# Hash attention and token mixing on one core: block sums moved ahead of the weight conversion, first loads moved behind the first hash bits, a square moved to a later step

## The chip, the core and the metric
The kernel runs on one core of one Trainium2 chip. The metric is the time of one execution on the device in microseconds (us), as a median over runs. A core has TensorE (PE: matrix products, with PEld for its weight loads), VectorE (DVE), ScalarE (ACT), GpSimd (POOL) and SyncE (SP), which here only issues DMA transfers. Each works through its own queue in order; they meet through semaphores.

## The reference, cut to what matters
Attention in which a query sees only keys of the same hash bucket, and behind it a mixer over tokens and channels:

```python
q_bits = (q @ proj > 0); k_bits = (k @ proj > 0)        # 6 bits each
mask = bucket(q_bits)[:, :, :, None] == bucket(k_bits)[:, :, None, :]
scores = where(mask, q @ k.T / sqrt(64), -1e9)
x = softmax(scores) @ v                                  # (4, 768, 8 heads * 64)
h = relu(x.T @ w_tok1) @ w_tok2                          # mixing over tokens
u = x + h.T
out = u + relu(u @ w_ch1) @ w_ch2                        # mixing over channels
```

Batch 4, 8 heads, 768 tokens, head dimension 64. The weights come as 64-bit numbers; the kernel turns their words into float32 itself.

## The kernel before
Two heads of one batch make a *pair*; there are 16 pairs, and a pair is done in two *halves* of 384 queries (`Half`). One (pair, half) is a *block* here. Keys come in six chunks of 128. Scores stand with the keys in the partitions, so that the sum over keys is a product with a matrix of ones.

A block on TensorE: `scores(0)` gives chunks 0 to 2 (`sc`, a product of q and k, and on top of it one of the hash bits, which makes the scores of other buckets hugely negative), `weigh(1)` is the older block's last three products with v (`acc`), `scores(1)` gives chunks 3 to 5, `weigh(0)` the first three products with v, and then the older block's `divide` makes its sums over keys (`sums`). ScalarE turns each chunk into `e` (exponential), sums up v for a small correction (`add_values`, tiles `vt`, `vsum`) and copies `acc` to `num`. The six `e` of a block are added before `sums`: GpSimd makes `esa` (e0 + e1); VectorE makes `esd` from e3, e4, e5 (`add(0)`) and then adds e2 and `esa` (`add(1)`). VectorE then takes the reciprocal `den` of `sums`, and GpSimd multiplies it with `num` into `XT`.

Once per pair, in its first half, `hashes(n + 1)` makes the next pair's bits: four products of q and k with `projblk` (`hp`), a comparison and a scaling on VectorE (`g`), and eight small DMAs that put the bits where the scores read them (`bits`). `hp` and `sums` share one PSUM buffer (tag `sm`, `bufs=1`), so the one product waits until VectorE has read the other.

From pair 1 on, each block also does one third of the conversion of a weight tile (`weights.some`): *begin* (ScalarE converts the low words, VectorE puts together `big` from the high words, two operations), *join* (one VectorE operation, ScalarE's square of the high words, two GpSimd products) and *end* (one VectorE operation, which writes the weight). Eight tiles are done in the attention, in blocks 2 to 25; with the thirds and halves the same step comes back after six blocks. The rest is converted in the mixer, where `weights.one` does all three steps in one call, the end being that of the tile before.

The order of each engine's work is the order of the code (`manual_schedule`). The loop that sets it is short:

```python
now.scores(0)
if before: before.weigh(1)
if half == 0: load(n + 2); hashes(n + 1)
if before: before.add(0)
now.scores(1)
if half == 0: add_values(n + 1)
if n: weights.some(third)
now.weigh(0)
if before: before.add(1); before.divide()
```

After the attention, `mix1(b)` turns x of batch b with transposes on TensorE (`trp`, two PSUM buffers) and copies on ScalarE (`turn`), and multiplies with `w_tok1` (`t`); `mix2(b)` multiplies with `w_tok2`, and VectorE adds into `XT`. From about 500 us on there is only the channel mixing.

Of the kernel before, what the change touches and what calls it, by code (L numbers as in the profile page):

```python
# [32 lines left out]
F32 = mybir.dt.float32  # L33
# [4 lines left out]
ALU = mybir.AluOpType  # L38
ACT = mybir.ActivationFunctionType
# [5 lines left out]
def kernel(  # L45
# [12 lines left out]
    nc = tc.nc  # L58
    P = 128
    B, NP, _, _, S = qk.shape  # L60
    D = 64
    NB = proj.shape[1]
# [7 lines left out]
    HALF = S // 2  # L70
# [6 lines left out]
    BIG = 2.0**20  # L77
# [10 lines left out]
    ones = const.tile([P, D], F32, name="ones")  # L88
    nc.vector.memset(ones, 1.0)

    projblk = const.tile([P, 32], F32, name="projblk")
    nc.vector.memset(projblk, 0.0)
    for i in range(2):
        nc.sync.dma_start(out=projblk[D * i : D * i + D, 16 * i : 16 * i + NB], in_=proj)


    bitscale = const.tile([P, 1], F32, name="bitscale")
    nc.gpsimd.memset(bitscale, BIG)
    nc.gpsimd.memset(bitscale[:64], 1.0)
    for j in range(2, 4):  # L100
        for i in range(2):
            nc.gpsimd.affine_select(
                out=bitscale, in_=bitscale, compare_op=ALU.not_equal, fill=-NB * BIG,
                base=-(32 * j + 16 * i + NB), pattern=[[0, 1]], channel_multiplier=1,
            )
    largest = const.tile([P, B * NP], F32, name="largest")
    unsafe = const.tile([1, 1], I32, name="unsafe")

# [14 lines left out]
    class Conversion:  # L123
# [48 lines left out]
        def join(self):  # L172
            if not self.begun:
                return
            raw, tmp, to, rows = self.begun
            self.begun = None
            lo, hi = raw[:, :, 0].bitcast(F32), raw[:, :, 1].bitcast(F32)
            big, unit = tmp[:, 0], tmp[:, 1]
            nc.vector.tensor_scalar(
                unit.bitcast(U32), big.bitcast(U32), 0xFF800000, None, op0=ALU.bitwise_and,  # L180
            )
            nc.scalar.activation(hi, hi, ACT.Square)
            nc.gpsimd.tensor_tensor(unit, unit, lo, op=ALU.mult)  # L183
            nc.gpsimd.tensor_tensor(big, big, unit, op=ALU.add)  # L184
            self.ready = hi, big, to, rows

        def end(self):

            if not self.ready:
                return  # L190
            size, big, to, rows = self.ready
            self.ready = None
            nc.vector.scalar_tensor_tensor(
                to, size.rearrange("p (t n) -> p t n", t=rows), LEAST * LEAST,
                big.rearrange("p (t n) -> p t n", t=rows), op0=ALU.is_ge, op1=ALU.mult,
            )
# [17 lines left out]
    pairs = [(b, hp) for b in range(B) for hp in range(NP)]  # L214

    def turn(b, x, bank):

        for r in range(0, NR, 2):
            ps = bank()
            for k in range(2):  # L220
                at = S * b + P * (r + k)
                for cb in range(NCB):
                    nc.tensor.transpose(ps[:, k, P * cb : P * cb + P], XT[:, cb, at : at + P], ident)
            nc.scalar.copy(x[:, r : r + 2], ps)


    def attention(pool, psum):
        zeroed = [pool.tile([P, 2, S], BF16, name=f"bits{n}", tag=f"bits{n}", bufs=1) for n in range(3)]
        loaded = {}

        def load(n):
            if n >= len(pairs):
                return
            b, hp = pairs[n]
            t = pool.tile([P, 2, S], F32, name="qk", tag="qk", bufs=3)
            if n:
                nc.sync.dma_start(out=t, in_=qk[b, hp])
            else:
                for half in range(2):
                    sl = slice(HALF * half, HALF * half + HALF)  # L240
                    nc.sync.dma_start(out=t[:, :, sl], in_=qk[b, hp, :, :, sl])
            vn = pool.tile([P, 2, NR, D], F32, name="vn", tag="vn", bufs=3)
            nc.sync.dma_start(out=vn, in_=v[b, hp])
            vt = pool.tile([P, S], F32, name="vt", tag="vt", bufs=2)
            nc.sync.dma_start(out=vt, in_=vT[b, hp])
            loaded[n] = [t, vn, vt, None]

        def add_values(n):

            vt = loaded[n][2]  # L250
            vsum = pool.tile([P, 1], F32, name="vsum", tag="vsum", bufs=4)
            nc.scalar.activation(vt, vt, ACT.Copy, scale=EPS, accum_out=vsum)
            loaded[n][3] = vsum

        def hashes(n):

            g = pool.tile([P, HALF], BF16, name="g", tag="g", bufs=2)
            ps = psum.tile([P, 512], F32, name="hp", tag="sm", bufs=1)
            for j in (0, 2, 1, 3):
                sl = slice(HALF * (j % 2), HALF * (j % 2) + HALF)  # L260
                nc.tensor.matmul(  # L261
                    ps[32 * j : 32 * j + 32, :HALF], projblk, loaded[n][0][:, j // 2, sl],
                    start=True, stop=True,
                )
            nc.vector.tensor_scalar(g, ps[:, :HALF], 0.0, 0.5, op0=ALU.is_gt, op1=ALU.subtract)
            nc.vector.tensor_scalar(g, g, bitscale, None, op0=ALU.mult)
            for j in (0, 2, 1, 3):
                sl = slice(HALF * (j % 2), HALF * (j % 2) + HALF)
                for i in range(2):
                    at = 32 * j + 16 * i  # L270
                    issuer = nc.scalar if n == 0 and j >= 2 else nc.sync
                    issuer.dma_start(
                        out=zeroed[n % 3][D * i : D * i + NB + 1, j // 2, sl], in_=g[at : at + NB + 1],
                    )

        def scores(n, half, chunks):
# [46 lines left out]
            at = S * b + HALF * half  # L323
            nc.gpsimd.tensor_tensor(XT[:, hp, at : at + HALF], num, den, op=ALU.mult)  # L324

        for n in range(2):
            load(n)
        for t in zeroed:
            nc.gpsimd.memset(t, 0.0)
        weights = Conversion(  # L330
            pool,
            [(w_tok1, W1, 3, (0, NR)), (w_tok2, W2, 1, (0, NJ)), (w_ch1, WC1, 1, (0, NCB // 2))],
            bufs=1,
        )
        hashes(0)
        add_values(0)
        half = None

        class Half:

# [7 lines left out]
            def weigh(self, g):  # L348
                if g == 0:
                    self.acc = psum.tile([P, 512], F32, name="acc", tag="acc", bufs=1)  # L350
                chunks = range(GR * g, GR * g + GR)
                weigh(self.n, self.acc, self.es[GR * g :], chunks)
                if g == 0:
                    self.a = pool.tile([P, 2, HALF], F32, name="esa", tag="esa", bufs=2)
                    nc.gpsimd.tensor_tensor(self.a, self.es[0], self.es[1], op=ALU.add)  # L355
                else:
                    self.num = pool.tile([P, HALF], F32, name="num", tag="num", bufs=3)
                    nc.scalar.activation(
                        self.num, self.acc[:, :HALF], ACT.Identity, bias=loaded[self.n][3],
                    )  # L360

            def add(self, k):

                es = self.es
                if k == 0:
                    self.d = pool.tile([P, 2, HALF], F32, name="esd", tag="esd", bufs=2)
                    nc.vector.tensor_tensor(self.d, es[3], es[4], op=ALU.add)  # L367
                    nc.vector.tensor_tensor(self.d, self.d, es[5], op=ALU.add)  # L368
                else:
                    nc.vector.tensor_tensor(self.d, self.d, es[2], op=ALU.add)  # L370
                    nc.vector.scalar_tensor_tensor(  # L371
                        self.d, self.d, NR * EPS, self.a, op0=ALU.add, op1=ALU.add,
                    )
# [6 lines left out]
        for n in range(len(pairs)):  # L380
            for half in range(2):
                now = Half(n, half)

                now.scores(0)
                if before:
                    before.weigh(1)
                if half == 0:
                    load(n + 2)
                    if n + 1 < len(pairs):
                        hashes(n + 1)  # L390
                if before:
                    before.add(0)

                now.scores(1)
                if half == 0 and n + 1 < len(pairs):
                    add_values(n + 1)
                if n:
                    weights.some(third)
                    third = (third + 1) % 3
                now.weigh(0)  # L400
                if before:
                    before.add(1)
                    before.divide()
                before = now
        while third or weights.fetched:
            weights.some(third)
            third = (third + 1) % 3
        before.weigh(1)
        before.add(0)
        before.add(1)  # L410
        turn(0, x0, lambda: psum.tile([P, 2, 512], F32, name="trp", tag="sc", bufs=3))
        before.divide()

# [231 lines left out]
```

## Time and profile before

| | us |
|---|---|
| median of three runs (lowest, highest) | 999.64 (999.03, 1001.22) |
| the profiled execution, its own time | 1003.09 |
| its span from first to last instruction | 1001.3 |
| TensorE busy | 946.6 (95%) |
| VectorE busy | 386.1 |
| ScalarE busy | 278.2 |
| GpSimd busy | 197.4 |
| mean granted clock of TensorE | 0.981 of full |

The span is that of one profiled execution, whose own time includes what lies around it. The profile names instructions by the line of the kernel (L285), the engine and the tiles. A wait is put down to the instruction that released it. A granted clock of 1.00 is 2.4 GHz and 0.50 is 1.2 GHz; a number between them is a mean over a stretch that had both.

### The profile page before, as it was taken

The page shows a single profiled execution, that of the slowest core. Times are in us where ns is not written, and L with a number is a line of the kernel's source. Part 1 is how long each engine was busy: PE and PEld are TensorE (multiplying, and loading weights), DVE is VectorE, ACT ScalarE, POOL GpSimd, SP SyncE. Part 2 cuts the span into 40 slices and gives each one's busy share as a digit, 9 for nine tenths or more (in the row PEclk, how much of TensorE's full clock was granted, in tenths as well). Part 3 has the DMA queues.
Part 4 walks back from the last instruction along what each step waited for, and adds up shares of the span by engine and source line. Part 5 has one row for each costly group of instructions (what it writes and reads, how often), then busy time and mean ns, then how long its engine had stood idle before and what let it go on. Part 6 is the DMA issues. An engine that isn't in the chain of part 4 may idle for free.

```text
span 1001.3 us, 9101 instructions
## 1 busy us (share of the span) xinstructions
PE 946.6 (95%) x3649; PEld 423.4 (42%) x3649; DVE 386.1 (39%) x349; ACT 278.2 (28%) x389; POOL 197.4 (20%) x119
## 2 busy tenths in 40 slices
PE   6998998999999997988999999999999999999997
PEld 2443343333333443445544444444444444444443
DVE  1577777777777787477400030020002003000000
ACT  3555554545554552433111011001001001100100
POOL 2144254334525232554200000000000000000000
PEclk8999999999999998998999999999999999999999
DMA  6121222232231011232000030030012003000000
GB/s 223 67 93 69 97 97 68 103 120 91 71 100 65 31 34 63 85 104 95 1 0 1 31 136 1 21 142 6 11 46 112 10 22 136 0 22 21 1 11 34
DMA packets 20513, 61.12 MB, mean 61 GB/s; under 512 B 2800, under 2 KB 4208, under 8 KB 20464
## 3 DMA queue, kind: packets, MB, share of 16 engines
q1 hardware_dynamic: 20408, 60.45, 17.3%
q8 instruction: 30, 0.49, 0.2%
q14 instruction: 19, 0.16, 0.1%
q10 hardware_dynamic: 56, 0.02, 0.0%
HBM read 53.48 MB, written 6.29 MB: 60 GB/s over the span
## 4 chain that ended last, share of the span: by engine, by line
PE 83%; DVE 12%; ACT 1%; issue 1%; DMA 1%; SPq 0%; DVEq 0%; ACTq 0%
PE c L552 25%; PE c L542 25%; PE sc L285 12%; PE acc L310 8%; PE t L513 5%; PE t L526 4%; PE sums L320 3%; DVE esd L371 3%; DVE den L322 2%; DVE esd L370 2%; DVE esd L368 2%; DVE tmp L164 1%; PE hp L261 1%; DVE tmp L167 1%; DVE esd L367 1%
## 5 line engine op out<-in xcount | busy, mean ns | idle before, releaser
L552 PE MATMUL c<-r,WC 128*128 128x512 f32 x576 | 248.2, 592 | 0.0
L542 PE MATMUL c<-XT,WC 128*128 128x512 f32 x576 | 248.2, 592 | 0.0
L302 ACT ACTIVATE e<-sc 128x768 f32<-128x768 f32 x192 | 153.1, 811 | 130.1 <-PE sc L285 128.1
L556 DVE TENSOR_TENSOR o<-c,XT 128x512 f32<-128x512 f32 x24 | 16.6, 692 | 425.4 <-PE c L552 425.4
L285 PE MATMUL sc<-qk 64*128 64x384 f32 x768 | 168.6, 519 | 0.0
L552 PEld LDWEIGHTS c<-r,WC 128*128 128x128 f32 x576 | 109.4, 190 | 137.8 <-issue 137.8
L542 PEld LDWEIGHTS c<-XT,WC 128*128 128x128 f32 x576 | 109.4, 190 | 137.1 <-issue 136.6
L547 ACT ACTIVATE r<-c 128x512 f32<-128x512 f32 x72 | 43.0, 598 | 430.4 <-PE c L542 430.4
L310 PE MATMUL acc<-e,vn 128*64 128x384 f32 x768 | 137.9, 494 | 0.0
L322 DVE RECIPROCAL den<-sums 128x384 f32<-128x384 f32 x32 | 81.9, 2558 | 47.8 <-PE sums L320 47.8
L285 PEld LDWEIGHTS sc<-qk 64*128 64x128 f32 x768 | 68.0, 194 | 71.2 <-issue 55.1
L310 PEld LDWEIGHTS acc<-e,vn 128*64 128x64 f32 x768 | 49.5, 136 | 76.4 <-issue 76.4
L324 POOL TENSOR_TENSOR XT<-num,den 128x384 f32<-128x384 f32 x32 | 40.7, 1272 | 197.0 <-ACT e L302 166.9
L355 POOL TENSOR_TENSOR esa<-e 128x768 f32<-128x768 f32 x32 | 66.4, 2076 | 19.3 <-ACT e L302 19.2
L285 PE MATMUL sc<-bits 64*128 64x384 bf16 x384 | 65.1, 332 | 4.7 <-DMA bits<-g 4.6
L183 POOL TENSOR_TENSOR tmp<-tmp,raw 128x768 f32<-128x768 f32 x20 | 44.0, 2202 | 68.7 <-ACT raw L162 32.4
L320 PE MATMUL sums<-esd,ones 128*64 128x384 f32 x128 | 27.5, 505 | 26.8 <-DVE esd L371 26.7
L513 PE MATMUL t<-x,W 128*128 128x512 f32 x96 | 47.3, 654 | 2.7 <-DVE den L322 2.7
L371 DVE SCALAR_TENSOR_TENSOR esd<-esd,esa 128x768 f32<-128x768 f32 x32 | 42.3, 1322 | 3.3
L184 POOL TENSOR_TENSOR tmp<-tmp 128x768 f32<-128x768 f32 x20 | 42.0, 2099 | 1.6
L368 DVE TENSOR_TENSOR esd<-esd,e 128x768 f32<-128x768 f32 x32 | 41.0, 1280 | 3.3
L526 PE MATMUL t<-W,r 128*128 128x384 f32 x128 | 41.8, 486 | 0.0
(44 smaller groups left out, 425.2 us busy)
## 6 DMA issues: line engine op xcount, KB each, us to landing
raw<-in_moe_w_ch SPq DMA_DIRECT2D x16, 768.0 KB
seen<-in_qk SPq DMA_DIRECT2D x16, 768.0 KB
qk<-in_qk SPq DMA_DIRECT2D x15, 768.0 KB
vn<-in_v SPq DMA_DIRECT2D x16, 384.0 KB
vt<-in_vT SPq DMA_DIRECT2D x16, 384.0 KB
out<-o SPq DMA_DIRECT2D x24, 256.0 KB
raw<-in_moe_w_tok SPq DMA_DIRECT2D x4, 768.0 KB
bits<-g SPq DMA_DIRECT2D x124, 5.2 KB
```

Of the source, the lines that this page charges most:

```text
L285: nc.tensor.matmul(sc[c][:, i, :HALF], t[rows, 1, P * c : P * c + P], t[rows, 0, qs], start=first, stop=not first,)
L302: nc.scalar.activation(e, sc[c][:, :, :HALF], ACT.Exp, scale=SCALE)
L310: nc.tensor.matmul(acc[D * i : D * i + D, :HALF], vn[:, i, c], e[:, i], start=(c == 0), stop=(c == NR - 1),)
L320: nc.tensor.matmul(ps[D * i : D * i + D, :HALF], ones, total[:, i], start=True, stop=True)
L322: nc.vector.reciprocal(den, ps[:, :HALF])
L355: nc.gpsimd.tensor_tensor(self.a, self.es[0], self.es[1], op=ALU.add)
L368: nc.vector.tensor_tensor(self.d, self.d, es[5], op=ALU.add)
L371: nc.vector.scalar_tensor_tensor(self.d, self.d, NR * EPS, self.a, op0=ALU.add, op1=ALU.add,)
L513: nc.tensor.matmul(ps, W1[:, r, P * j : P * j + P], x[:, r], start=(r == 0), stop=(r == NR - 1),)
L526: nc.tensor.matmul(ps[:, :HALF], r1[:, j, P * cb : P * cb + P], W2[:, j, HALF * half : HALF * half + HALF], start=(j == 0), stop=(j == NJ ...
L542: nc.tensor.matmul(ps, WC1[:, cb, P * t : P * t + P], XT[:, cb, sl], start=(cb == 0), stop=(cb == NCB - 1),)
L552: nc.tensor.matmul(ps, WC2[:, t, P * cb : P * cb + P], r2[t], start=(t == 0), stop=(t == NHT - 1),)
```

## The change
Four things move; no arithmetic changes.

- In a block, the four adds of the older block's `esd` come ahead of the weight step: the two of `add(1)` (formerly `add(0)`) behind `weigh(1)`, the two of `add(2)` behind `scores(1)`. GpSimd's `esa`, now `add(0)`, is issued behind `scores(1)` too, ahead of GpSimd's part of the weight step.
- `hashes(n + 1)` comes behind the weight step instead of behind `weigh(1)`.
- At the start, `projblk` is issued by ScalarE behind a first small exponential (`warm`), the loads of v for pair 0 and all loads for pair 1 come behind pair 0's hash bits, and pair 0's bits are made and issued in two parts, first those of the first half of the tokens.
- ScalarE's square of the high words moves from *join* to *end*.

```diff
-        nc.sync.dma_start(out=projblk[D * i : D * i + D, 16 * i : 16 * i + NB], in_=proj)
+        nc.scalar.dma_start(out=projblk[D * i : D * i + D, 16 * i : 16 * i + NB], in_=proj)
...
         # Conversion.join
-            nc.scalar.activation(hi, hi, ACT.Square)
             nc.gpsimd.tensor_tensor(unit, unit, lo, op=ALU.mult)
             nc.gpsimd.tensor_tensor(big, big, unit, op=ALU.add)
...
         # Conversion.end
             self.ready = None
+            nc.scalar.activation(size, size, ACT.Square)
             nc.vector.scalar_tensor_tensor(
...
         # hashes
-            for j in (0, 2, 1, 3):
-                sl = slice(HALF * (j % 2), HALF * (j % 2) + HALF)
+            for j in range(4):
+                sl = slice(HALF * (j // 2), HALF * (j // 2) + HALF)
...
-            nc.vector.tensor_scalar(g, ps[:, :HALF], 0.0, 0.5, op0=ALU.is_gt, op1=ALU.subtract)
-            nc.vector.tensor_scalar(g, g, bitscale, None, op0=ALU.mult)
+            for rows in [slice(0, 64), slice(64, P)] if n == 0 else [slice(0, P)]:
+                nc.vector.tensor_scalar(
+                    g[rows], ps[rows, :HALF], 0.0, 0.5, op0=ALU.is_gt, op1=ALU.subtract,
+                )
+                nc.vector.tensor_scalar(g[rows], g[rows], bitscale[rows], None, op0=ALU.mult)
...
-                    issuer = nc.scalar if n == 0 and j >= 2 else nc.sync
+                    issuer = nc.scalar if n == 0 and i else nc.sync
...
-        for n in range(2):
-            load(n)
+        warm = pool.tile([P, 1], F32, name="warm", tag="warm", bufs=1)
+        nc.scalar.activation(warm, ones[:, :1], ACT.Exp)
+        load_qk(0)
         for t in zeroed:
             nc.gpsimd.memset(t, 0.0)
+        hashes(0)
+        load_v(0)
+        load_qk(1)
+        load_v(1)
+        add_values(0)
...
-        hashes(0)
-        add_values(0)
...
                 now.scores(0)
                 if before:
                     before.weigh(1)
+                    before.add(1)
                 if half == 0:
-                    load(n + 2)
-                    if n + 1 < len(pairs):
-                        hashes(n + 1)
-                if before:
-                    before.add(0)
+                    load_qk(n + 2)
+                    load_v(n + 2)
                 now.scores(1)
+                if before:
+                    before.add(2)
+                now.add(0)
                 if half == 0 and n + 1 < len(pairs):
                     add_values(n + 1)
                 if n:
                     weights.some(third)
                     third = (third + 1) % 3
+                if half == 0 and n + 1 < len(pairs):
+                    hashes(n + 1)
                 now.weigh(0)
                 if before:
-                    before.add(1)
                     before.divide()
```

VectorE in a first half with an *end* step, before and then after the change (`esd` are the adds, `W_86` and `W_87` the weight that the step writes, `g` the hash bits):

```order
L322 RECIPROCAL den<-sums 128x384
L265 TENSOR_SCALAR g<-hp 128x384
L266 TENSOR_SCALAR g<-g,bitscale 128x384
L367 TENSOR_TENSOR esd<-e 128x768
L368 TENSOR_TENSOR esd<-esd,e 128x768
L193 SCALAR_TENSOR_TENSOR W_86<-raw,tmp 128x768
L370 TENSOR_TENSOR esd<-esd,e 128x768
L371 SCALAR_TENSOR_TENSOR esd<-esd,esa 128x768
```

```order
L329 RECIPROCAL den<-sums 128x384
L378 TENSOR_TENSOR esd<-e 128x768
L379 TENSOR_TENSOR esd<-esd,e 128x768
L381 TENSOR_TENSOR esd<-esd,e 128x768
L382 SCALAR_TENSOR_TENSOR esd<-esd,esa 128x768
L195 SCALAR_TENSOR_TENSOR W_87<-raw,tmp 128x768
L270 TENSOR_SCALAR g<-hp 128x384
L273 TENSOR_SCALAR g<-g,bitscale 128x384
```

The hash bits went from the front of the block to its end, and the weight step from between the adds to behind them.

ScalarE in the mixer, from the second call of `one` in `mix2(0)` to the copies of x for batch 2, before and then after (`raw` are the words of a tile; L162 and L164 convert the low ones, L182 and L194 square the high ones):

```order
L162 ACTIVATE raw_2954<-raw_2954 128x768
L182 ACTIVATE raw_2954<-raw_2954 128x768
L162 ACTIVATE raw_2973<-raw_2973 128x768
L182 ACTIVATE raw_2973<-raw_2973 128x768
L224 COPY x0_89<-trp_3029 128x1024
```

```order
L164 ACTIVATE raw_2958<-raw_2958 128x768
L194 ACTIVATE raw_2908<-raw_2908 128x768
L164 ACTIVATE raw_2977<-raw_2977 128x768
L194 ACTIVATE raw_2958<-raw_2958 128x768
L226 COPY x0_90<-trp_3033 128x1024
```

The last square ahead of the copies was that of the tile just begun, and is now that of the tile before it.

SyncE's transfers at the start, before and then after:

```order
L241 DMA qk<-in_qk 128x2x384
L94 DMA projblk<-in_proj 64x6 x2
L241 DMA qk<-in_qk 128x2x384
L243 DMA vn<-in_v 128x768
L245 DMA vt<-in_vT 128x768
L237 DMA qk<-in_qk 128x1536
L243 DMA vn<-in_v 128x768
L245 DMA vt<-in_vT 128x768
L151 DMA raw<-in_moe_w_tok 128x3x512
L272 DMA bits_99<-g 7x384 x4
```

```order
L239 DMA qk<-in_qk 128x2x384 x2
L279 DMA bits_100<-g 7x384 x4
L247 DMA vn<-in_v 128x768
L249 DMA vt<-in_vT 128x768
L239 DMA qk<-in_qk 128x1536
L247 DMA vn<-in_v 128x768
L249 DMA vt<-in_vT 128x768
L153 DMA raw<-in_moe_w_tok 128x3x512
```

The four bits that SyncE issues for pair 0 stood behind six further loads and a weight, and now stand in front of them; `projblk` is gone from this queue.

## Rows read from the trace of the kernel before
**Rows 1.** Waits of TensorE: for whom, us in total, times, longest.
```profile
PE sums L320 <- DVE esd L371: 26.7, 19, 2.6
```
**Rows 2.** Busy time of each engine in stretches (start:end, length), granted clock, DMA.
```profile
34.37:382.16 347.79, 323.54 (x2032) 137.71 (x2034) 260.70 (x210) 185.71 (x254) 138.44 (x76) 0.98 0.23 78
...
362.14:372.20 10.06, 10.06 (x67) 4.46 (x65) 8.34 (x5) 5.40 (x7) 4.00 (x2) 1.00 0.00 0
166.43:178.19 11.76, 11.76 (x67) 5.18 (x65) 9.25 (x6) 5.45 (x7) 6.50 (x4) 0.85 0.26 83
```
**Rows 3.** The chain that ended last, 36 to 42 us: start, us, what.
```profile
39.08 0.78 PE hp L261 x8
```
**Rows 4.** VectorE in order of time, of three blocks: start, us, instruction, idle before.
```profile
39.93 0.56 DVE L265 TENSOR_SCALAR g<-hp 128x384 bf16<-128x384 f32 x1 [2.95 <-PE hp L261]
...
42.69 0.56 DVE L164 TENSOR_SCALAR tmp<-raw 128x768 uint32<-128x768 uint32 x1
43.28 0.96 DVE L167 SCALAR_TENSOR_TENSOR tmp<-raw,tmp 128x768 uint32<-128x768 uint32 x1
...
138.34 0.95 DVE L193 SCALAR_TENSOR_TENSOR W<-raw,tmp 128x768 f32<-128x768 f32 x1
...
379.96 0.96 DVE L371 SCALAR_TENSOR_TENSOR esd<-esd,esa 128x768 f32<-128x768 f32 x1
```
**Rows 5.** TensorE in order of time, end of pair 15's first half.
```profile
371.45 0.81 PE L320 MATMUL sums<-esd,ones 128*64 128x384 f32 x4
```
**Rows 6.** GpSimd in order of time, a block with a join.
```profile
125.64 2.44 POOL L183 TENSOR_TENSOR tmp<-tmp,raw 128x768 f32<-128x768 f32 x1 [1.42 <-ACT num L358]
```
**Rows 7.** ScalarE in order of time, in pair 1's first half and in the mixing.
```profile
43.29 0.83 ACT L252 ACTIVATE vt<-vt 128x768 f32<-128x768 f32 x1
...
434.97 0.92 ACT L182 ACTIVATE raw<-raw 128x768 f32<-128x768 f32 x1 [4.72 <-DVE tmp L167]
```
**Rows 8.** TensorE in order of time, in the token mixing.
```profile
409.85 1.09 PE L223 MATMUL trp<-ident,XT 128*128 128x128 f32 x8 [1.44 <-ACT x L224]
410.78 10.46 PE L513 MATMUL t<-x,W 128*128 128x512 f32 x24
...
436.82 1.97 PE L223 MATMUL trp<-ident,XT 128*128 128x128 f32 x8 [3.51 <-ACT x L224]
438.59 11.18 PE L513 MATMUL t<-x,W 128*128 128x512 f32 x24
...
467.12 12.26 PE L513 MATMUL t<-x,W 128*128 128x512 f32 x24
```
**Rows 9.** TensorE in order of time, at the start.
```profile
5.16 3.10 PE L261 MATMUL hp<-qk,projblk 128*32 128x384 f32 x8 [5.16 <-DMA projblk<-in_proj]
...
18.93 1.52 PE L285 MATMUL sc<-qk 64*128 64x384 f32 x4
```
**Rows 10.** SyncE's queue in order of time, at the start.
```profile
1.53 1.22 SPq L94 DMA_DIRECT2D projblk<-in_proj  x2
2.79 0.60 SPq L241 DMA_DIRECT2D qk<-in_qk  x1
...
20.54 5.90 SPq L272 DMA_DIRECT2D bits<-g  x8
```
**Rows 11.** ScalarE in order of time, at the start.
```profile
12.99 1.28 ACT L252 ACT_TABLE_LOAD   x1 [12.99 <-DMA bits<-g]
14.29 0.84 ACT L252 ACTIVATE vt<-vt 128x768 f32<-128x768 f32 x1
...
16.95 2.21 ACT L302 ACTIVATE e<-sc 128x768 f32<-128x768 f32 x3 [1.73 <-PE sc L285]
```
**Rows 12.** TensorE's weight loads in order of time, at the start.
```profile
6.77 0.19 PEld L261 LDWEIGHTS hp<-qk,projblk 128*32 128x32 f32 x4 [1.43 <-DMA qk<-in_qk]
```
**Rows 13.** Busy time of each engine from 10 to 14 us; last, DMA share and GB/s.
```profile
10.00:14.00 4.00, 1.25 (x8) 0.38 (x4) 0.00 (x0) 1.01 (x1) 0.00 (x0) 0.92 1.02 401
```
**Rows 14.** The chain that ended last, 4 to 17 us.
```profile
12.67 3.73 DMA bits<-g
```

More of the change, by code (lines that the diff above doesn't have):

```diff
@@ L93 @@
     for i in range(2):
-        nc.sync.dma_start(out=projblk[D * i : D * i + D, 16 * i : 16 * i + NB], in_=proj)
+        nc.scalar.dma_start(out=projblk[D * i : D * i + D, 16 * i : 16 * i + NB], in_=proj)
     bitscale = const.tile([P, 1], F32, name="bitscale")
     nc.gpsimd.memset(bitscale, BIG)
[L99 to L105, printed above, removed]
+    for j in range(4):
+        if j % 2 == 0:
+            nc.gpsimd.memset(bitscale[32 * j : 32 * j + 32], 1.0)
+        else:
+            for i in range(2):
+                nc.gpsimd.affine_select(
+                    out=bitscale, in_=bitscale, compare_op=ALU.not_equal, fill=-NB * BIG,
+                    base=-(32 * j + 16 * i + NB), pattern=[[0, 1]], channel_multiplier=1,
+                )
     largest = const.tile([P, B * NP], F32, name="largest")
@@ L229, in attention, with load_qk @@
         loaded = {}
-        def load(n):
+        def load_qk(n):
             if n >= len(pairs):
@@ L235, in load, with load_v @@
             t = pool.tile([P, 2, S], F32, name="qk", tag="qk", bufs=3)
[L236 to L241, printed above, removed]
+            for sl in [slice(0, HALF), slice(HALF, S)] if n == 0 else [slice(0, S)]:
+                nc.sync.dma_start(out=t[:, :, sl], in_=qk[b, hp, :, :, sl])
+            loaded[n] = [t, None, None, None]
+        def load_v(n):
+            if n >= len(pairs):
+                return
+            b, hp = pairs[n]
             vn = pool.tile([P, 2, NR, D], F32, name="vn", tag="vn", bufs=3)
@@ L258, in hashes @@
             ps = psum.tile([P, 512], F32, name="hp", tag="sm", bufs=1)
-            for j in (0, 2, 1, 3):
-                sl = slice(HALF * (j % 2), HALF * (j % 2) + HALF)
+            for j in range(4):
+                sl = slice(HALF * (j // 2), HALF * (j // 2) + HALF)
                 nc.tensor.matmul(
-                    ps[32 * j : 32 * j + 32, :HALF], projblk, loaded[n][0][:, j // 2, sl],
+                    ps[32 * j : 32 * j + 32, :HALF], projblk, loaded[n][0][:, j % 2, sl],
                     start=True, stop=True,
                 )
-            nc.vector.tensor_scalar(g, ps[:, :HALF], 0.0, 0.5, op0=ALU.is_gt, op1=ALU.subtract)
-            nc.vector.tensor_scalar(g, g, bitscale, None, op0=ALU.mult)
-            for j in (0, 2, 1, 3):
-                sl = slice(HALF * (j % 2), HALF * (j % 2) + HALF)
+            for rows in [slice(0, 64), slice(64, P)] if n == 0 else [slice(0, P)]:
+                nc.vector.tensor_scalar(
+                    g[rows], ps[rows, :HALF], 0.0, 0.5, op0=ALU.is_gt, op1=ALU.subtract,
+                )
+                nc.vector.tensor_scalar(g[rows], g[rows], bitscale[rows], None, op0=ALU.mult)
+            for j in range(4):
+                sl = slice(HALF * (j // 2), HALF * (j // 2) + HALF)
                 for i in range(2):
                     at = 32 * j + 16 * i
-                    issuer = nc.scalar if n == 0 and j >= 2 else nc.sync
+                    issuer = nc.scalar if n == 0 and i else nc.sync
                     issuer.dma_start(
-                        out=zeroed[n % 3][D * i : D * i + NB + 1, j // 2, sl], in_=g[at : at + NB + 1],
+                        out=zeroed[n % 3][D * i : D * i + NB + 1, j % 2, sl], in_=g[at : at + NB + 1],
                     )
@@ L334, in attention @@
         )
-        hashes(0)
-        add_values(0)
-        half = None
         class Half:
@@ L352, in weigh @@
                 weigh(self.n, self.acc, self.es[GR * g :], chunks)
[L353 to L356, printed above, removed]
+                if g == 1:
                     self.num = pool.tile([P, HALF], F32, name="num", tag="num", bufs=3)
@@ L365, in add @@
                 if k == 0:
+                    self.a = pool.tile([P, 2, HALF], F32, name="esa", tag="esa", bufs=2)
+                    nc.gpsimd.tensor_tensor(self.a, es[0], es[1], op=ALU.add)
+                elif k == 1:
                     self.d = pool.tile([P, 2, HALF], F32, name="esd", tag="esd", bufs=2)
@@ L386, in attention @@
                     before.weigh(1)
+                    before.add(1)
                 if half == 0:
-                    load(n + 2)
-                    if n + 1 < len(pairs):
-                        hashes(n + 1)
+                    load_qk(n + 2)
+                    load_v(n + 2)
+                now.scores(1)
                 if before:
-                    before.add(0)
-                now.scores(1)
+                    before.add(2)
+                now.add(0)
                 if half == 0 and n + 1 < len(pairs):
@@ L408, in attention @@
         before.weigh(1)
-        before.add(0)
         before.add(1)
+        before.add(2)
         turn(0, x0, lambda: psum.tile([P, 2, 512], F32, name="trp", tag="sc", bufs=3))
```

2 lines of the change are left out of this document (1 added, 1 removed).

## The prediction
> **What bounds the kernel now.** I read in this order: the waits of TensorE, the stretches between block starts, VectorE's, GpSimd's and ScalarE's rows inside a block, the token mixing, and the start. TensorE is the engine of the chain nearly everywhere; from 500 us on it hardly pauses, so only its idle time before that can be won. Its longest sum of waits is 26.7 us, in 19 waits of the `sums` products for VectorE's last add [rows 1].
>
> A *block* is one (pair, half). An undisturbed one lasts 10.06 us [rows 2]; with the hash products of the next pair, 0.78 [rows 3], it is 10.84. From pair 1 to the last products of pair 15, 34.37 to 382.16, are 347.8 us [rows 2]. Undisturbed they would be 14 halves with hashes at 10.84 and 16 without at 10.06, 312.7 in all. So 35.1 us are waits and what follows them: after some waits TensorE is granted 0.85 of its clock over a block, which then lasts 11.76, 1.7 more [rows 2]; a part of it runs at 1.2 GHz.
>
> **Why the sum is late.** In a first half VectorE sits idle 2.95 us for the hash products although the older block's exponentials lie ready; then come hash bits, two adds, a weight operation, two adds [rows 4]. All four adds must end before `sums`.
>
> **The new order in a block, pairs 1 to 12.** I count from the start of a block's scores. VectorE does the reciprocal, then all four adds at once. What that costs with GpSimd's work in between can be read: in the last pair no weight is converted and no hash waits, so its second half already runs reciprocal and four adds in this order, collisions with GpSimd included. There the last add ends at 379.96 + 0.96 = 380.92, in a block begun at 372.20: 8.7 us in [rows 2, 4]. `sums` begins at 371.45, 0.75 before the next block [rows 5, 2], so it is due at 9.3 in a second half and 10.1 in a first. The adds end in time, and what may now hold `sums` is the comparison of the hash products (L270): both use one PSUM buffer, and the comparison stands behind the weight operation. By thirds:
> - First half, *begin*: two word operations, 1.55 [rows 4], to 10.2; the comparison 0.56 [rows 4], to 10.75. `sums` waits 0.65.
> - First half, *join*: one short operation; the comparison ends before 10.1. No wait. But GpSimd now starts two products, the first 2.44 [rows 6]; the scaling of the bits waits for it, so the next reciprocal starts 0.7 late, and the following second half runs some 0.2 over.
> - First half, *end*: L195 now needs ScalarE's square from the same block. ScalarE does three exponentials, then `vt`, which starts at 43.29, 8.9 in; 0.78 of this was for hash products that now come later [rows 7, 3], so 8.1, to 9.0. The square takes 0.92 [rows 7], to 10.0; L195 0.95, to 11.0; the comparison to 11.6 [rows 4]. `sums` waits 1.55.
> - Second halves: 8.7 against 9.3, no wait but the 0.2 above. Their weight operation falls into VectorE's idle time before the next reciprocal.
>
> Six blocks hold each third once in a first and once in a second half: 0.65 + 1.55 + 0.2 = 2.4. Four such rounds are 9.6. In pairs 13 to 15, 8.7 plus 0.56 is before 10.1: no wait. So 347.8 becomes 312.7 + 9.6 = 322.3, **25.5 less.** Bounds: 35 if none of the new waits shows; 10 if the eight waits of the first halves are twice as long (8.8) and four of them cost the slower clock (6.8). I take the middle, since it is made of rows that already hold the new order.
>
> **Squares in the mixing.** Now ScalarE's square of a word waits 4.7 us for VectorE's L167, which reads the same words [rows 7]; the copies of the transposed `x` queue behind it, and TensorE's third bank of transposes waits 3.5 for them [rows 8]. This happens twice alike, for x of batches 2 and 3. After the change the square is that of the call before, whose words L167 has read long since, and the copies start as soon as the first bank is full: 2 x 3.5, less 0.2. The eight transposes behind the wait take 1.97 where they took 1.09, and 24 products 11.18 and 12.26 for 10.46 [rows 8]: 2 x 0.88 + 0.72 + 1.80 = 4.3 more. Batch 1's wait of 1.44 [rows 8] stays, for a square is still queued at that place. **11.1 less.** What grows: the last word operation waits for the square, and the first adds of `mix2` stand behind it, some 2 us later than now; four PSUM banks cover that. If they don't, it costs 1 to 3. Bounds 7 to 11; nothing at all is a rival below.
>
> **The start.** `projblk` now comes from ScalarE behind a table load and an activation. It was used at 5.16 [rows 9], 2.4 after its last issue's end (1.53 + 1.22) [rows 10]. An estimate: ScalarE's load from 0.75, 1.28 long [rows 11], an activation of 0.2, two issues of some 0.75, so 3.7, and 2.4 more: 6.1. The hash products take 3.1 [rows 9]; their first half's bits can be issued from 8.7 on, the last ones until 11.6, and no longer queue behind loads. But `vn` and `vt` of pair 0 are issued behind them, and ScalarE's first exponential stands behind `vt`'s sum. A load of 384 KB took 4.0 from issue (2.79) to use (6.77) [rows 10, 12]; one more of that size takes 1.0 at 401 GB/s [rows 13]. Issued from 11.65, `vt` is there at 16.7, its sum (0.84) ends at 17.6, and the exponentials start at 17.75 where they started at 16.95 [rows 11]. TensorE goes on at 18.55, 0.4 before the 18.93 of now [rows 9], with 2.6 of scores and then 0.8 of hash products, which now precede those scores. It will have stood idle some 5 us, as now, and then its clock was half. Between 0.2 gained (full clock) and 2.2 lost (half clock throughout) I take **1.5 lost**, because the idle stretch is as long as that of now.
> The Trainium skill ("ScalarE: Activation LUTs", *What ACT_TABLE_LOAD costs*) puts a drain of about 1.38 us behind a load of 1.28. By it the start would lose 2.9 and the kernel take 1.4 more. The trace shows the 1.28, but the next activation at 14.29, 0.02 after the load's end, so no drain there [rows 11].
>
> **Sum.** 25.5 + 11.1 - 1.5 = 35.1. The profiled execution took 1003.1, 3.5 above the median of three runs, 999.6; no stage here explains this difference, so I take the 35.1 from both: 968.0 for a profile, **964.5 as a median.** About 0.2% (2 us) can be told from no change.
>
> **Rivals.**
> - *The waits come back in another place* (15%): the new waits of 1.55 drop the clock each time, or VectorE and GpSimd collide otherwise than in pair 15. For it: the slow block of [rows 2] stood behind a wait. Against it: the adds, which caused the waits, have 0.6 to 1.4 us in hand. Price 6.8 for the clock alone, 15.6 with the waits doubled: 971 to 980, say 974.
> - *The mixing gains nothing* (10%): the word operation behind the square holds the adds, and so PSUM, as long as the copies waited before. 975.6.
> - *The table load holds ScalarE longer* (5%): by one more stretch of 1.28, which delays `projblk` and all behind it. 965.8.
> - *The hash bits come too late* (4%), the way to a slower kernel. They are now issued at the end of a first half, not in its middle. After a *join* their scaling ends 11.65 in; the last of eight issues (5.9 in all) starts 5.2 later [rows 10], 16.85 in, and the slowest landing that the chain shows is 3.73 from issue [rows 14]. That is 20.6, or 9.8 into the second half. The next pair's scores need them there at 10.06 + 0.75, a margin of 1.0. To eat the gain, each of 15 pairs would have to wait 35/15 = 2.3, so the bits would have to land 3.3 later than I reckon. Then 1000 and more, say 1005.
> - *No effect* (3%): what held the adds were not VectorE's places but exponentials or GpSimd. Against it the 8.7 of pair 15. 999.6.
> - *No new wait shows* (3%): 955.
>
> **Numbers.** The likeliest (60%) is 964.5, itself between 958 and 971. Range 955 to 979; it leaves out the two cases without a gain and the tails. Faster by over 0.2%: 60 + 15 + 10 + 5 + 3 = 93%; same 3%; slower 4%.
>
> **What would show it.** After the change: waits of `sums` for VectorE near 10 us in place of 26.7, nearly all for the comparison of hash products, in first halves with *begin* or *end*; second halves of 10.1; one wait of transposes for ScalarE, of 1.4; the first exponential near 17.8, released by `vt`. I am wrong where TensorE's scores wait for bits at a pair's start, where `sums` still waits for the adds, or where the adds of `mix2` hold the products of `t`.

## The result, and the profile after

The changed kernel takes 967.99 us (median of 4 runs, 967.04 to 968.95), the kernel before 999.34 in the runs beside it: a ratio of 0.968, with a 95% interval of 0.967 to 0.970. Forecast were 964.5 and a range of 955 to 979. The gain is 31.4 us in the medians; between the two profiled executions (1003.09 and 967.04) it is 36.0, where 35.1 was forecast.

TensorE's waits after the change. A row names the engine, its line and tile, the releaser, and then the sum, the number of waits and the longest:

```profile
PE sums L327 <- DVE g L270: 6.7, 8, 1.3
PE hp L265 <- DMA projblk<-in_proj: 6.0, 1, 6.0
PE sc L292 <- ACT e L309: 5.6, 1, 5.6
...
PE sums L327 <- DVE esd L382: 2.6, 1, 2.6
PE trp L225 <- ACT x L226: 1.9, 3, 1.4
PE t L539 <- DVE XT L545: 0.9, 2, 0.7
```

The 26.7 us of waits for the last add [rows 1] have become 2.6, a single wait, in the tail behind the last pair; the kernel before has that one too. New are eight waits for the comparison of the hash products (L270). The waits of the transposes for ScalarE have shrunk from 8.5 to 1.9.

The stretches that answer to [rows 2]: first six blocks from pair 1 on, then all from pair 1 to pair 15's last products, then the token mixing. The columns are busy time and instructions of PE, PEld, DVE, ACT and POOL, then the granted clock, the DMA share and GB/s:

```profile
35.05:46.53 11.48, 11.06 (x74) 4.53 (x72) 10.56 (x9) 7.06 (x10) 4.00 (x2) 1.00 0.26 88
46.53:56.60 10.07, 10.07 (x67) 4.46 (x65) 8.82 (x6) 5.40 (x7) 4.82 (x3) 1.00 0.19 62
56.60:68.91 12.31, 11.06 (x74) 4.53 (x72) 10.34 (x8) 7.03 (x10) 7.00 (x4) 1.00 0.23 85
68.91:78.98 10.07, 10.07 (x67) 4.47 (x65) 9.74 (x7) 6.24 (x8) 4.02 (x2) 1.00 0.39 139
78.98:89.82 10.84, 10.84 (x74) 4.61 (x72) 10.56 (x9) 6.23 (x9) 5.60 (x3) 1.00 0.29 94
89.82:99.95 10.13, 10.13 (x68) 4.53 (x66) 9.53 (x7) 6.22 (x8) 6.08 (x4) 1.00 0.02 4
35.05:356.26 321.21, 314.52 (x2034) 135.51 (x2034) 290.20 (x210) 186.67 (x254) 150.10 (x76) 1.00 0.25 85
367.33:464.54 97.21, 94.41 (x297) 51.27 (x298) 73.50 (x79) 33.49 (x41) 53.55 (x25) 0.97 0.24 73
```

The first halves hold *begin*, *end* and *join* in this order. Over 10.84 they run 0.64, 1.47 and 0.00; the second half after the *join* runs 0.07 over 10.06. The waits are a little shorter than that (6.7 in eight): in the two blocks that run over, TensorE is also busy for 11.06 where 10.84 would do. The clock stays at 1.00: none of these waits was followed by a slow block. VectorE in the 12.31 block, by start and length, and ScalarE's square (L194):

```profile
56.72 2.56 DVE L329 RECIPROCAL den<-sums 128x384 f32<-128x384 f32 x1 [1.00 <-PE sums L327]
59.19 1.14 DVE L378 TENSOR_TENSOR esd<-e 128x768 f32<-128x768 f32 x1
...
64.60 0.96 DVE L382 SCALAR_TENSOR_TENSOR esd<-esd,esa 128x768 f32<-128x768 f32 x1
66.64 0.96 DVE L195 SCALAR_TENSOR_TENSOR W<-raw,tmp 128x768 f32<-128x768 f32 x1 [1.08 <-ACT raw L194]
67.51 0.55 DVE L270 TENSOR_SCALAR g<-hp 128x384 bf16<-128x384 f32 x1
65.63 0.90 ACT L194 ACTIVATE raw<-raw 128x768 f32<-128x768 f32 x1
```

The adds end 8.96 into the block (8.7 forecast). L195 then stands 1.08 us for the square of its own block, and behind it the comparison ends at 68.06, which releases `sums`.

### The profile page after: what moved, and what is told of

Same layout as the page of the kernel before. It is cut to its first block, busy times and chain, and to the rows that moved or that the text cites. A ratio compares the mean times of both kernels' runs of the same rounds, so it can differ in the third digit from the quotient of the medians.

```text
span 965.3 us, 9061 instructions
## 1 busy us (share of the span) xinstructions
PE 932.7 (97%) x3649; PEld 418.5 (43%) x3649; DVE 425.4 (44%) x351; ACT 279.8 (29%) x390; POOL 214.3 (22%) x120
## 4 chain that ended last, share of the span: by engine, by line
PE 82%; DVE 10%; ACT 4%; issue 2%; DMA 1%; SPq 0%; DVEq 0%; ACTq 0%
PE c L565 26%; PE c L555 26%; PE sc L292 14%; PE acc L317 10%; PE sums L327 2%; ACT e L309 2%; DVE tmp L169 2%; PE t L526 2%; PE t L539 2%; DVE tmp L166 1%; DVE den L329 1%; DVE WC L195 1%; DVE esd L381 1%; DVE esd L379 1%; ACT raw L194 1%
## 5 line engine op out<-in xcount | busy, mean ns | idle before, releaser
L292 PE MATMUL sc<-qk 64*128 64x384 f32 x768 | 164.7, 508 | 5.6 <-ACT e L309 5.6
L331 POOL TENSOR_TENSOR XT<-num,den 128x384 f32<-128x384 f32 x32 | 49.1, 1535 | 166.0 <-ACT e L309 150.0
L375 POOL TENSOR_TENSOR esa<-e 128x768 f32<-128x768 f32 x32 | 79.4, 2482 | 19.8 <-ACT e L309 19.8
L381 DVE TENSOR_TENSOR esd<-esd,e 128x768 f32<-128x768 f32 x32 | 75.5, 2360 | 1.1
L379 DVE TENSOR_TENSOR esd<-esd,e 128x768 f32<-128x768 f32 x32 | 50.1, 1565 | 2.8
L526 PE MATMUL t<-x,W 128*128 128x512 f32 x96 | 44.6, 623 | 2.7 <-DVE den L329 2.7
L185 POOL TENSOR_TENSOR tmp<-tmp 128x768 f32<-128x768 f32 x20 | 39.4, 1972 | 1.6
L577 DVE TENSOR_REDUCE largest<-seen 128x1 f32<-128x1536 f32 x16 | 28.0, 1753 | 26.0 <-DMA seen<-in_qk 25.1
```

Source lines behind the costliest of these rows:

```text
L292: nc.tensor.matmul(sc[c][:, i, :HALF], t[rows, 1, P * c : P * c + P], t[rows, 0, qs], start=first, stop=not first,)
L375: nc.gpsimd.tensor_tensor(self.a, es[0], es[1], op=ALU.add)
L526: nc.tensor.matmul(ps, W1[:, r, P * j : P * j + P], x[:, r], start=(r == 0), stop=(r == NR - 1),)
```

## The experiments

Each kernel was timed beside the kernel before on its chip (998.7, 999.95 and 999.5 in the three batches); a number of us "less" is against that. Comparisons with the changed kernel are across batches, so differences of 1 or 2 us there say little.

**The square alone** (on the kernel before).

```diff
         # join
-            nc.scalar.activation(hi, hi, ACT.Square)
...
         # end
+            nc.scalar.activation(size, size, ACT.Square)
```

> The kernel before with one edit: the square moved from join to end. Theory: the gain of the token mixing stands by itself, 9.4 us as between the two profiles, and the attention changes by less than 2 us (the end step's wait for the square falls into first halves only where the adds already wait). So 988 to 991 where before is 999.5; one wait of transposes for ScalarE is left, of 1.4. Rival (the gain in the mixing is borrowed: it came from the mixing starting in another phase of loads and of GpSimd's work): within 3 us of before.

It took 1026.16, ratio 1.025 [1.022, 1.028]: 27 us more, a plain miss. TensorE's waits, and VectorE's waits for the square at the first four of the eight tiles:

```profile
PE sums L320 <- DVE esd L371: 44.3, 19, 3.7
PE trp L223 <- ACT x L224: 1.9, 3, 1.4
DVE W L193 <- ACT raw L192: 15.1, 4, 5.3
```

and one *end* on VectorE:

```profile
147.57 0.96 DVE L193 SCALAR_TENSOR_TENSOR W<-raw,tmp 128x768 f32<-128x768 f32 x1 [2.32 <-ACT raw L192]
148.44 0.95 DVE L370 TENSOR_TENSOR esd<-esd,e 128x768 f32<-128x768 f32 x1
149.50 0.96 DVE L371 SCALAR_TENSOR_TENSOR esd<-esd,esa 128x768 f32<-128x768 f32 x1
```

The mixing gained as forecast: the waits of `trp` fall from 8.5 to 1.9, and it takes 97.26 (427.28 to 524.54), as in the changed kernel. But the attention from pair 1 on takes 381.53 (34.00 to 415.53), 34 more than in the first profile of before. There the old order has two adds behind the last word operation, and that now waits 2.3 to 5.4 us for ScalarE in each of the eight *ends*. Slower-clock stretches come on top: TensorE is busy 339.77 us of this stretch where it was 323.54 [rows 2], and the mean granted clock of the execution is 0.966 (0.981 and 0.989 in two profiles of the kernel before). The late square needs the adds to stand ahead of it.

**The order of the blocks alone**: adds first, hash bits behind the weight step, in the short form of the loop; GpSimd's `esa` moves into `add(0)` as in the change.

```diff
                 now.scores(0)
                 if before: before.weigh(1)
+                if before: before.add(1)
-                if half == 0: hashes(n + 1); before.add(0)
                 now.scores(1)
+                if before: before.add(2)
+                now.add(0)
                 weights.some(third)
+                if half == 0: hashes(n + 1)
                 now.weigh(0)
-                before.add(1)
                 before.divide()
```

> The kernel before with the block order alone: adds ahead of the weight step, hash products behind it; start and square as before. Theory: the stretch of pairs 1 to 15 loses all of the 26.6 us and some more, since the end step of a first half no longer waits for a square of its own block: the wait of 1.5 in these four blocks falls to about 0.1, so 30 to 33 us less by the profile and 26 to 31 by the median; the mixing still has its three waits for ScalarE. Rival (the square moved late is part of what freed VectorE in the block): 20 us or less.

It took 970.41 (0.971 [0.968, 0.973]): 28.3 less, nearly the whole of the gain. From pair 1 on the attention takes 316.53 (34.87 to 351.40). Its waits:

```profile
PE trp L223 <- ACT x L224: 8.5, 3, 3.5
PE sums L320 <- DVE esd L371: 2.6, 1, 2.6
PE sums L320 <- DVE g L265: 1.7, 4, 0.4
```

**The adds alone, and the hash bits alone.** The first takes from the edit above the lines on the adds, with `hashes` in its old place ahead of them; the second takes those on `hashes`.

> The kernel before with the adds alone moved ahead of the weight step; the hash products stay behind weigh(1), so VectorE still waits 2.95 us for them. Theory: in first halves the four adds start at 6.5 and end near 10.5, so sums waits 0.4 to 0.6 in 15 first halves, 6 to 9 us in all, and nothing in second halves; 20 to 25 us faster than before. Rival (the idle time for the hash products is the cause): 10 us or less faster.

> The kernel before with the hash products alone moved behind the weight step; the adds stay on both sides of it. Theory (the adds ahead of the weight step carry the gain): VectorE does two adds early, but the last two now stand behind the comparison of the hash products, which cannot start before 8.1 us into the block; they end near 11.0, where sums is due at 10.1. So first halves still wait about 1 us each, 10 to 16 us of waits of sums for the adds are left of 26.8, and the kernel is 5 to 12 us faster than before. Rival (VectorE's idle 2.95 us for the hash products is the whole cause): 20 us or more faster.

Adds first: 975.24 (0.976 [0.974, 0.978]), 24.7 less. Hash bits late: 1002.35 (1.0017 [1.0003, 1.003]), 2.4 more and no gain, which I had not expected. The wait for the last add in each:

```profile
PE sums L320 <- DVE esd L371: 8.2, 15, 2.6
```

```profile
PE sums L320 <- DVE esd L371: 27.4, 19, 3.1
```

VectorE with the hash bits late, in a first half with a *join*, shows why:

```profile
157.36 0.56 DVE L265 TENSOR_SCALAR g<-hp 128x384 bf16<-128x384 f32 x1 [2.62 <-PE hp L261]
157.96 0.78 DVE L266 TENSOR_SCALAR g<-g,bitscale 128x384 bf16<-128x384 bf16 x1
158.66 2.56 DVE L370 TENSOR_TENSOR esd<-esd,e 128x768 f32<-128x768 f32 x1
```

The idle time of 2.95 in front of the first adds [rows 4] is gone, but 2.62 of it has come back in front of the last two. In first halves with *begin* and *end* only 0 and 0.61 come back, but there a word operation that lasted 0.57 and 0.95 lasts 2.16 and 2.56, and the waits for the last add are 27.4 in all where they were 26.7. The hash bits pay only once all adds are ahead of them: 28.3 less in place of 24.7, and the waits of `sums` ahead of the tail fall from 5.6 in 14 to 1.7 in 4.

**The start alone.** Loads, `projblk`, the order of the first bits and `warm` as in the change, all else as before (the diff is that part of the change's).

> The kernel before with the start alone: projblk issued by ScalarE behind a first exponential, loads behind the first hash bits, bits in two parts. Theory: no gain; the first exponential stands near 17.2 (16.95 before), pair 1 begins 0 to 1 us later, the median is within 2 us of before. Rival (the earlier bits are worth something, and the after kernel loses it to its hash products of pair 1 ahead of the first products with v): 2 us or more faster.

1002.6 (1.003 [1.0009, 1.005]), 3.9 more, a small miss. With the old place of the hash step its products for pair 1 wait for the load that was moved back, and pair 1 starts at 37.55 (34.37 before):

```profile
PE hp L265 <- DMA qk<-in_qk: 7.4, 1, 7.4
```

**The kernel before once more**, to see how far two profiles of one kernel differ.

> The kernel before, unchanged, for a second profile. Theory on the size: the profiled execution of before (1003.1) was above the median because in it more waits were followed by a lower clock than in a usual one; the blocks that last 11.7 instead of 10.1 are others here, or fewer, and the time goes with their number at 1.7 each. At a time near 999.5 there are two fewer of them. Rival (the profiler itself costs before 3.5 us): again about 1003 with the same blocks slow.

996.14, against 1003.09 for the first; the 39 other executions of this kernel on record lie between the two, from 996.78 to 1002.67. The waits of `sums` are the same (26.8 in 19). The same two stretches as [rows 2] and the mixing:

```profile
33.74:378.66 344.92, 320.50 (x2035) 136.29 (x2034) 260.72 (x210) 185.48 (x254) 138.51 (x76) 0.99 0.23 79
389.73:493.20 103.47, 94.96 (x296) 52.28 (x297) 63.92 (x79) 33.03 (x41) 48.32 (x25) 0.96 0.21 69
```

In the first profile they are 347.79 at a mean clock of 0.98 and 106.63 at 0.92:

```profile
393.23:499.86 106.63, 98.16 (x296) 54.02 (x297) 63.94 (x79) 32.97 (x41) 48.40 (x25) 0.92 0.20 67
```

So 6 of the 7 us between them lie in these two stretches, where TensorE has the same waits and is busy longer at a lower granted clock.

**Is the square what holds the first-half ends?** The changed kernel with the square in *join* during the attention and late only in the mixer.

```diff
         # join
+            if self.bufs == 1:
+                nc.scalar.activation(hi, hi, ACT.Square)
...
         # end
-            nc.scalar.activation(size, size, ACT.Square)
+            if self.bufs > 1:
+                nc.scalar.activation(size, size, ACT.Square)
```

> The changed kernel with the square back in the join during the attention, and in the next block's hash step only in the mixing. Theory (in the attention the late square is what the last word step of a first-half end waits for, and the adds behind it cost 1.47 us in each of four such blocks): those waits fall to 0.4 or below, the stretch of attention is some 4 to 5 us shorter than in the changed kernel, the mixing keeps its length of 97, and the time is 962.5 to 964. Rival (the last word step ends late for another reason, such as the adds themselves lasting longer beside GpSimd's sums): the first-half ends keep their wait, and the time is within 1 us of the changed kernel.

963.77 (0.963 [0.961, 0.966]), 4.2 less than the changed kernel. The block with the *end*, then the whole stretch:

```profile
57.67:68.76 11.09, 11.02 (x74) 4.52 (x72) 10.25 (x8) 6.15 (x9) 6.99 (x4) 1.00 0.28 102
36.11:352.63 316.52, 314.51 (x2034) 135.51 (x2034) 289.14 (x210) 186.71 (x254) 150.09 (x76) 1.00 0.25 86
```

12.31 has become 11.09, and the stretch is 4.7 shorter. The rival falls: VectorE's adds last as long as in the changed kernel, and nearly all of the excess is gone with the square. The stretch is also that of the blocks alone (316.53), which have the old square too.

**The hash bits between the adds and the weight step** (on the changed kernel).

```diff
+                if half == 0: hashes(n + 1)
                 weights.some(third)
-                if half == 0: hashes(n + 1)
```

> The changed kernel with the next pair's hash products behind the adds and ahead of the weight step. Theory: the comparison ends near 9.3 in every first half and no longer stands behind the weight step, so the waits of sums in first halves with begin (0.64) and end (1.47 by the length of the blocks) go, four times each: 8.4 us less than the changed kernel, 959 to 960.5. Rival (the weight step, now last in VectorE's block, delays the reciprocal and with it the next block): 4 us less or nothing.

961.4 (0.962 [0.960, 0.965]), 6.6 less than the changed kernel. No wait for `g` is left; the stretch takes 314.73:

```profile
PE sums L327 <- DVE esd L382: 3.7, 5, 2.6
```

Four second halves, those behind a *join*, wait 0.17 to 0.39 for the last add, which I had not reckoned with; the time is 0.9 above the range expected.

**The first v sum later**, behind pair 0's first exponentials.

```diff
-        add_values(0)
...
+                if n == 0 and half == 0:
+                    add_values(0)
                 if half == 0 and n + 1 < len(pairs):
                     add_values(n + 1)
```

> The changed kernel with ScalarE's sum of v for pair 0 behind its first three exponentials instead of ahead of them. Theory: the exponentials start when the bits' products end, near 11.8 in place of 17.16; TensorE's wait of 5.6 goes, and the next limit is the load of pair 1's q and k for its hash products, which is in about 18.6, so the first products with v start near 19.5 to 20.5 in place of 22.9: 2 to 4 us less than the changed kernel, 964 to 966. Rival (the loads of v and of pair 1 decide the start whatever ScalarE does): within 1 us of the changed kernel.

966.72 (0.967 [0.965, 0.970]), only 1.3 less than the changed kernel, which can't be told from nothing: a miss. By the profiles pair 1 starts 0.5 earlier (34.59). ScalarE's exponentials start at 12.3 in place of 17.2, but TensorE then stops at pair 1's load and comes back at about half the clock (0.55 granted from 20.80 to 24.50):

```profile
20.02 0.85 PE L265 MATMUL hp<-qk,projblk 128*32 128x384 f32 x8 [4.18 <-DMA qk<-in_qk]
20.80 3.76 PE L317 MATMUL acc<-e,vn 128*64 128x384 f32 x12
```

**Both, with pair 1's load first.** The two edits above, and `load_qk(1)` ahead of `load_v(0)`.

```diff
         hashes(0)
-        load_v(0)
         load_qk(1)
+        load_v(0)
         load_v(1)
```

> The changed kernel with three moves: the hash step of the next block stands between the adds and the weight step, as in the run with hashes before the weights (961.4); the v sum of the first pair stands behind its first exponentials; and the load of pair 1's q and k is issued ahead of the load of the first pair's v. Theory (the start is held by pair 1's load, which landed near 20.0 where the v sum was moved alone): the load lands near 17, the hash products of pair 1 run there, the first v products follow near 18 at the full clock, and pair 1's keys start near 30 to 31, against 35.05 in the changed kernel and 34.6 with the v sum moved alone; 955 to 957 us. Rival (the v load then lands late and the v products wait for it, or the clock there is low whatever stands ahead): pair 1 starts at 34 or later, 960 or more.

955.48 (0.955 [0.952, 0.957]): 12.5 less than the changed kernel. The same two rows as above:

```profile
16.72 0.85 PE L265 MATMUL hp<-qk,projblk 128*32 128x384 f32 x8 [0.90 <-DMA qk<-in_qk]
17.59 2.16 PE L317 MATMUL acc<-e,vn 128*64 128x384 f32 x12
```

The wait is 0.90 in place of 4.18, the twelve products take 2.16 in place of 3.76, and pair 1 starts at 29.74 (35.05 in the changed kernel); from there the stretch is 314.76. The move of the load was not run by itself.

## Why the prediction was right, and what was off

**Attention, 25.5 forecast, 26.6 measured** (347.79 to 321.21). That the four adds follow each other and end in time holds (8.7 and 8.96 into two first halves). The new excess of the blocks came by thirds as reckoned: 0.65, 1.55 and 0.2 forecast, 0.64, 1.47 and 0.07 measured. The mechanism of the largest is shown by the experiment that puts the square back: 4.7 us in the stretch, which the late square costs in the attention. The new order by itself is worth 31.3 there (347.79 to 316.53). The step **"Why the sum is late"** named two things, the idle 2.95 and the adds behind the weight operation; alone, the adds give 24.7 and the idle time nothing.

In one thing the bounds were too wide. They allowed for clock drops behind the new waits, up to 6.8; there were none in the six blocks shown, and the granted clock of the whole stretch is 1.00.

**Mixing, 11.1 forecast, 9.6 measured** (106.63 to 97.05; the row of 97.21 above runs 0.16 past the first product of the channel mixing, at 464.38). The term was mis-sized, not its mechanism. TensorE's rows after the change:

```profile
407.38 1.09 PE L225 MATMUL trp<-ident,XT 128*128 128x128 f32 x8 [0.23 <-ACT x L226]
424.09 5.43 PE L539 MATMUL t<-W,r 128*128 128x384 f32 x16 [0.16 <-DVE XT L545]
431.49 1.09 PE L225 MATMUL trp<-ident,XT 128*128 128x128 f32 x8 [0.23 <-ACT x L226]
```

The two waits of 3.5 [rows 8] are 0.23 each, 6.6 less. The products of `mix2` now wait 0.16 and 0.74 for the adds into `XT`, the growth that the step set at nothing because of four PSUM banks, and one of the signs that it had named for being wrong. With the products behind these waits `mix2` takes 1.4 longer (10.75 for 10.32 and 21.65 for 20.64). The products behind the two old waits ran at the full clock, 4.2 less where 4.3 was forecast.

But those 4.2 are not the same in every execution. Six profiles on record have the old squares, with the same 8.5 of waits of `trp`. In three of them the mixing takes 106.3 to 106.7: the kernel before, the start alone (393.99 to 500.67) and the hash bits late (390.98 to 497.27). In three it takes 103.5 to 103.6: the kernel before again, the blocks alone (363.02 to 466.65) and the adds alone (368.09 to 471.70). With the late squares it takes 96.6 to 97.3 in all six profiles. So the change gains 6.4 to 9.6 here, 8 in the mean: 5.2 are the waits less the 1.4, and the rest comes from the clock.

**Start, 1.5 lost forecast, 0.7 measured** (34.37 to 35.05; 1.3 against the second profile of before). ScalarE's and TensorE's first rows:

```profile
0.74 1.28 ACT L335 ACT_TABLE_LOAD   x1 [0.74 <-PEq L646]
1.01 1.36 ACTq L94 DMA_DIRECT2D projblk<-in_proj  x2
2.04 0.20 ACT L335 ACTIVATE warm<-ones 128x1 f32<-128x1 f32 x1
16.32 0.84 ACT L256 ACTIVATE vt<-vt 128x768 f32<-128x768 f32 x1 [14.08 <-DMA vt<-in_vT]
5.96 1.51 PE L265 MATMUL hp<-qk,projblk 128*32 128x384 f32 x8 [5.96 <-DMA projblk<-in_proj]
18.00 1.65 PE L292 MATMUL sc<-qk 64*128 64x384 f32 x4 [5.58 <-ACT e L309]
```

The order of events is as forecast: products near 6.1 (5.96), `vt` near 16.7 (16.3), its sum ahead of the exponentials, and TensorE idle some 5 us for them (5.58). Two premises were wrong. This step, like the list of changes, puts the issues of `projblk` behind the first activation. In the code they stand ahead of `warm` (L94 and L335), and they go out at 1.01, inside the load. And the hash products took 1.51, not 3.1 [rows 9]; the 3.1 held a wait of 1.43 for a load of q and k [rows 12]. The 6.1 came out near by chance: the issues ended at 2.37 and not 3.7, and the use came 3.6 behind that and not 2.4. Of the drain behind the load (the Trainium skill, "ScalarE: Activation LUTs", *What ACT_TABLE_LOAD costs*) this trace shows nothing either: the load ends at 2.02 and the next activation begins at 2.04.

**The sum.** Between the two profiles 26.6 + 9.6 - 0.7 and 0.5 behind the mixing are 36.0; 35.1 was forecast. The step that failed is **"so I take the 35.1 from both"**. The first profile of before held more slow-clock stretches than most executions of that kernel: its mean granted clock is 0.981, where the 35 that were timed beside the experiments have 0.981 to 0.987. Many of those bunch near 998.5 us at 0.985 and near 1002.4 at 0.982, some 4 apart; that this is the long and the short mixing is likely, but not shown, as they left no trace. The first profile's mixing was one of the three long ones, and its attention, 347.79, is 2.9 and 2.4 above two other profiles with the old blocks (344.92 for the kernel before again, 345.38 for the start alone). What such stretches cost belongs to that execution and not to the median, so the median gained 31.4. Of the 4.7 between that and 36.0, 3.75 are the first profile's distance above the median of before, and 0.95 are the changed kernel's profile below its own median. Against the second profile of before the gain is 29.1 (23.7 in the attention, 6.4 in the mixing, 0.3 behind it, less 1.3 at the start); the median's lies between the two. Why the clock falls behind a wait in one execution and not in another stays open. I had called the 3.5 us between profile and median unexplained and gone on as though they did not touch the saving.

*The mixing gains nothing* falls with the 6.4, and *the table load holds ScalarE longer* with the issue at 1.01. *The waits come back in another place* falls with the clock of 1.00, and *no new wait shows* with the eight waits of `sums`. The rivals *hash bits too late* and *no effect* find nothing in the trace: TensorE's scores wait 0.2 us in all for bits, and once.

## What to carry to other kernels

Edits on one in-order queue have no prices of their own: here the square alone cost 27 us, the hash bits alone gave nothing, the adds alone gave 24.7, and the whole change gave 31. Put first on a queue what another engine waits for, and check what the next wait is at that place. Take several profiles of the kernel before: waits that all of them show can be counted in full, and time lost to the clock only by its mean over them. Here the mixing loses 106.6 - 103.5 = 3.1 us more in one profile than in the next, behind the same waits.

## What the hardware showed that was not expected

- Two executions of the kernel before, with the same waits (26.7 and 26.8 us of `sums`), differ by 7 us, 6 of them because the granted clock fell in different places: 0.92 against 0.96 of full over the mixing. Over six profiles with the old squares the mixing takes either some 103.5 or some 106.5.
- ScalarE's DMA issues go out while it loads a table (from 1.01 to 2.37, the load from 0.74 to 2.02).
- An add of 0.95 us on VectorE takes 2.45 when it meets GpSimd's add. VectorE and GpSimd in the first block of pair 1:

```profile
40.24 2.45 DVE L381 TENSOR_TENSOR esd<-esd,e 128x768 f32<-128x768 f32 x1
39.35 2.52 POOL L375 TENSOR_TENSOR esa<-e 128x768 f32<-128x768 f32 x1
```

  GpSimd's add begins first and ends at 41.87; VectorE's ends 0.82 later, at 42.69, about the length of an add by itself. The Trainium skill ("SBUF — State Buffer", *SBUF: two separate sides*) says that GpSimd and an operation of VectorE with two inputs in SBUF share a port pair, which goes wholly to the one that starts first; the two rows agree. It didn't decide the time here, since the last adds still ended in time.
